# Row maxima turned as fp32, small steps of the norm on GpSimd, and repeated probabilities in 64-row halves: one change to a four-layer attention kernel

## The chip, the cores and the metric

The kernel runs on one core of one Trainium2 chip. A core has TensorE (PE, matrix products into PSUM), VectorE (DVE), ScalarE (ACT), GpSimd (POOL) and SyncE (SP, which here only issues DMAs). Each works through its own queue in order and they meet at semaphores. The metric is device microseconds for the whole program, the median of several executions; lower is better.

## What is computed

The reference applies four layers in turn, A, B, A, B, to x of 2048 tokens and 512 features. Each layer normalises its input, attends with 32 heads of 16 features, projects and adds. A looks at 8 keys per token, every second one back; B at the last 256 keys.

```python
def _A_ref(x, wqkv, wo):
    W, dil = 8, 2
    ...
    logits = jnp.einsum("bhsd,bhswd->bhsw", q, kg) * scale
    logits = jnp.where(mask[None, None, :, :], logits, -1e9)
    attn = _softmax(logits, axis=-1)
    o = jnp.einsum("bhsw,bhswd->bhsd", attn, vg)

def _B_ref(x, wqkv, wo):
    ...
    H = 32; Dh = D // H; W = 256
    ...
    mask = (idx[:, None] - idx[None, :] >= 0) & (idx[:, None] - idx[None, :] < W)
    scores = jnp.where(mask[None, None], scores, -1e9)
    p = _softmax(scores, axis=-1)
    o = jnp.einsum("bhqk,bhkd->bhqd", p, v)

x = A_x
x = x + _A_ref(_layernorm(x, axis=-1), A_wqkv, A_wo)
x = x + _B_ref(_layernorm(x, axis=-1), B_wqkv, B_wo)
x = x + _A_ref(_layernorm(x, axis=-1), A_wqkv, A_wo)
x = x + _B_ref(_layernorm(x, axis=-1), B_wqkv, B_wo)
```

Products are carried out as sums of three fp16 products: each operand is split into a high half (`xh`, `wh`) and the rest (`xl`, `wl`).

## The kernel before

The tokens are cut into 8 chunks of 256 (`C`). A chunk passes `layer_a` and `layer_b` twice, 16 pairs in all, named A0, B0 to A15, B15. Nothing is issued where it is written: `plan.add` records a task with its engine, its estimated time, the values it reads and writes, and a label of TensorE's tiling (`mode`: F the whole array, R halves of 64 rows, C strips of 32 columns, H strips of 32 rows). Each task has a number from the table `ORDER`, one list per scope. `Plan.order` sorts each engine's tasks by these numbers, so the table is the order of every engine's queue. A negative number -1-p means: the other engine named by `alt`, at place p. At each time two or three neighbouring chunks are under way together, and the table interleaves them. The scope W holds 110 tasks of three idle matmuls that only keep TensorE busy.

The tasks that matter here, with their lines:

- `norm` (L742 to L773), 32 times: VectorE takes mean and variance of both 128-token halves and adds epsilon (`stats`, three instructions per half, the last L744), GpSimd raises to the power -0.5 (`rstd`, L747), VectorE makes the shift (`shift`, L750), ScalarE normalises (`xnorm`, L763), TensorE turns the result (L767), ScalarE takes the high half (L772), VectorE the low half (L773).
- the projections: L792 to L794 (turned, `pq`), L811 to L813 (`pv` and the output `po`).
- `layer_a`: VectorE multiplies keys and queries (`prod`, L921, `alt` GpSimd), TensorE sums over the features (L929, strips of columns), a softmax follows. `spread` (L988) repeats each probability over 8 features with a 0/1 matrix `selt`: a task of four matmuls of 32 rows and 512 columns, two per output tile, four tasks per chunk. `weigh` (L1001, VectorE) multiplies with the values, `total` (L1008 to L1010 on GpSimd, L1006 on VectorE as `alt`) sums over the 8 keys. Task n of `spread` serves the 128-token half n // 2.
- `finish`: high and low half of the output (L831 ScalarE, L833 GpSimd or VectorE), the output projection, the addition to x (L839).
- `layer_b`: for each of four groups j of heads, eight times: scores of queries against keys (`sq`, L1096 and L1099, halves), then masked copy (L1115) and maximum over the keys (L1117) on VectorE. Then the maxima are split into two fp16 halves (`msplit`, L1126 and L1127, VectorE), turned on TensorE (`mrow`, L1131), copied out of PSUM (L1140, VectorE) and put by two DMAs (`mput`, L1136) into rows 48 and 49 of each half of the query stack `stk`, so that the second scores (`sk`, L1169 and L1171) come with the maximum already subtracted. ScalarE takes the exponential (L1175), GpSimd masks (L1184), TensorE multiplies with the values (`av`, L1201, strips of columns), ScalarE empties PSUM (L1236). The score tiles `sq` and `sk` share a PSUM pool of two buffers; the other PSUM tiles share four (`q_pj`).

These lines of `Plan.add` and `Plan.order` set the order of every queue:

```python
t.place, t.alt = ORDER[self.scope][self.k] if self.scope in ORDER else len(self.tasks), alt
if t.place < 0:
    (t.eng, t.us), t.place = alt, -1 - t.place
...
for q in queue.values():
    q.sort(key=lambda t: t.place, reverse=True)
```

Of the kernel before, what the change touches and what calls it, by code (L numbers as in the profile page):

```python
# [9 lines left out]
F16 = mybir.dt.float16  # L10
BF16 = mybir.dt.bfloat16
F32 = mybir.dt.float32
# [516 lines left out]
def kernel(  # L529
# [29 lines left out]
    for name, bufs in (("q_sc", 2), ("q_pj", 4)):  # L559
        pool(name, bufs, bass.MemoryType.PSUM)  # L560
    ctx.enter_context(tc.manual_schedule())


    idf = cst.tile([P, P], F32, name="idf")
    make_identity(nc, idf)
    idh = cst.tile([P, P], F16, name="idh")
    nc.vector.tensor_copy(idh, idf)
    ones = cst.tile([1, P], F32, name="ones")
    nc.gpsimd.memset(ones, 1.0)
    mhalf = cst.tile([P, 2], F32, name="mhalf")  # L570
    nc.gpsimd.memset(mhalf, -0.5)

# [777 lines left out]
```

## Time and profile before

| | |
|---|---|
| time, median of 3 executions | 1518.68 us (1513.79 to 1522.99) |
| span of the profiled execution, first to last instruction | 1515.1 us |
| time of the profiled execution around its span | not listed |
| VectorE's rows of `norm` that the diff removes (L744, L750) | 96 instructions |
| VectorE's rows of the maxima that the diff removes (L1126, L1127, L1140) | 192 instructions |
| TensorE's rows of the spreads (L988) | 256 instructions |
| TensorE's rows of the turned maxima (L1131) | 128 instructions |

How to read the lines that follow in the prediction. A row of the groups of instructions names the line, the engine, the operation, output<-input, the shapes and the count; then come the busy time in us, the mean of one in ns, and after the second bar the idle time of the engine just before them with what ended it. A row of a tile's view has minimum, median and maximum in ns. A row of the waits has the waiting engine and line, what it waited for, the total in us, how often, and the longest. A row of the timeline has the start in us, the duration, engine, line and operation. PE's matmuls overlap in the pipeline, so the step from one start to the next tells more than the duration of one.

### The profile page before, as it was taken

What the parts mean: (1) busy time and instruction counts of PE and PEld (TensorE: products, weight loads), DVE (VectorE), ACT (ScalarE), POOL (GpSimd) and SP (SyncE); (2) the same over time, 40 slices, a digit from 0 to 9 for tenths busy, and PEclk for the clock granted to TensorE, in tenths of its full rate; (3) what the DMA queues carried; (4) which work ended last, traced back from release to release, by engine and by line L of the source; (5) the groups of instructions that cost most, each with busy time, mean ns of one, the idle gap of its engine ahead of it and who ended that gap; (6) DMA issues with size and microseconds to landing.
All of it is one profiled execution on the core that took longest, in us unless ns stands there. A gap on an engine that the chain in (4) does not pass through costs nothing.

```text
span 1515.1 us, 35124 instructions
## 1 busy us (share of the span) xinstructions
PE 1394.5 (92%) x14186; PEld 793.1 (52%) x14186; DVE 1257.6 (83%) x2361; ACT 732.5 (48%) x1011; POOL 695.4 (46%) x783
## 2 busy tenths in 40 slices
PE   6899989989898998989999998999989899898988
PEld 4574636546374553736446363645637365463544
DVE  6968797987979888897988869798897979889774
ACT  6522445455455554455545344544544555445554
POOL 2504163463726356172452727255372735628232
PEclk9898989999999998999999898998999999999999
DMA  6030211222121221222112122212212121121221
GB/s 236 15 97 23 69 47 56 56 61 75 41 87 37 70 56 53 78 52 77 45 52 77 39 87 52 84 38 60 79 41 85 33 88 48 57 77 40 77 53 44
DMA packets 73091, 96.34 MB, mean 64 GB/s; under 512 B 17120, under 2 KB 44256, under 8 KB 72928
## 3 DMA queue, kind: packets, MB, share of 16 engines
q1 hardware_dynamic: 72672, 93.83, 21.5%
q8 instruction: 111, 1.82, 0.5%
q14 instruction: 52, 0.43, 0.1%
q10 hardware_dynamic: 256, 0.26, 0.1%
HBM read 49.81 MB, written 34.05 MB: 55 GB/s over the span
## 4 chain that ended last, share of the span: by engine, by line
PE 56%; DVE 19%; POOL 7%; issue 6%; ACT 5%; DMA 4%; SPq 3%; ACTq 0%; POOLq 0%; DVEq 0%
PE pq L792 9%; PE pq L793 7%; PE pq L794 7%; PE av L1201 6%; DVE m L1117 5%; PE sk L1169 4%; ACT p L1175 4%; PE L L929 3%; DVE sq L1115 3%; PE po L811 3%; PE sq L1096 3%; PE po L813 2%; PE po L812 2%; POOL pw L1008 2%; PE sq L1099 2%
## 5 line engine op out<-in xcount | busy, mean ns | idle before, releaser
L1175 ACT ACTIVATE p<-sk,sclB 128x768 f32<-128x768 f32 x480 | 426.6, 900 | 297.5 <-PE sk L1171 278.3
L1184 POOL TENSOR_SCALAR_AFFINE_SELECT p<-p 128x1024 f32<-128x1024 f32 x240 | 266.6, 1116 | 499.4 <-ACT p L1175 455.5
L1117 DVE TENSOR_REDUCE m<-sq 128x2 f32<-128x512 f32 x448 | 310.4, 693 | 15.4
L1115 DVE COPY_PREDICATED sq<-maskt,sq 128x256 f32<-128x256 int16 x448 | 188.8, 421 | 81.4 <-PE sq L1099 74.7
L1201 PE MATMUL av<-p,v 128*32 128x128 f32 (+1 forms) x3840 | 202.6, 334 | 7.4 <-POOL p L1184 7.3
L921 DVE TENSOR_TENSOR pr<-kv,q 128x512 f32<-128x512 f32 x223 | 167.4, 807 | 35.4 <-ACT q L900 17.1
L1169 PE MATMUL sk<-stk,stk 64*128 64x256 f16 x960 | 138.2, 287 | 36.8 <-DVE m L1117 20.2
L1201 PEld LDWEIGHTS av<-p,v 128*32 128x32 f32 x3840 | 109.0, 110 | 93.7 <-issue 33.3
L1001 DVE TENSOR_TENSOR pw<-pb,kv 128x1024 f32<-128x1024 f32 x128 | 153.1, 1214 | 4.0 <-POOL o L1010 1.7
L1008 POOL TENSOR_TENSOR pw<-pw 128x512 f32<-128x512 f32 x104 | 132.7, 1276 | 25.1 <-DVE pw L1001 24.4
L1096 PE MATMUL sq<-stk,stk 48*128 48x128 f16 (+1 forms) x896 | 114.5, 255 | 32.0 <-DVE m L1117 17.8
L1099 PE MATMUL sq<-stk,stk 48*128 48x256 f16 (+1 forms) x1024 | 128.4, 252 | 8.5 <-DVE m L1110 3.6
L1169 PEld LDWEIGHTS <-stk 64*128 64x128 f16 x960 | 53.3, 94 | 156.4 <-issue 99.4
L1096 PEld LDWEIGHTS <-stk 48*128 48x128 f16 x896 | 50.0, 95 | 123.1 <-issue 78.8
L1171 PE MATMUL sk<-stk,stk 64*128 64x128 f16 x960 | 109.3, 223 | 0.0
L763 ACT ACTIVATE xn<-x,rs 128x512 f32<-128x512 f32 x64 | 52.0, 813 | 80.9 <-DVE rs L750 72.9
L1009 POOL TENSOR_TENSOR pw<-pw 128x256 f32<-128x256 f32 x104 | 76.3, 734 | 8.2
L921 POOL TENSOR_TENSOR pr<-kv,q 128x512 f32<-128x512 f32 x33 | 46.5, 1415 | 58.7 <-PE L L929 36.0
L929 PE MATMUL L<-pr,sel 128*32 128x512 f32 x512 | 70.6, 601 | 0.9 <-DVE pr L921 0.7
L792 PE MATMUL pq<-xh,wA0h 128*128 128x256 f16 x256 | 70.9, 277 | 0.4 <-DVE el L1032 0.4
L792 PE MATMUL pq<-xh,wB0h 128*128 128x256 f16 x256 | 70.2, 274 | 1.0 <-DVE el L1032 1.0
L792 PE MATMUL pq<-xh,wA2h 128*128 128x256 f16 x256 | 70.6, 276 | 0.0
(183 smaller groups left out, 3159.9 us busy)
## 6 DMA issues: line engine op xcount, KB each, us to landing
stk<-re SPq DMA_DIRECT2D x256, 96.0 KB
re<-eh SPq DMA_DIRECT2D x128, 128.0 KB
re<-el SPq DMA_DIRECT2D x64, 128.0 KB
oc<-os SPq DMA_DIRECT2D x120, 64.0 KB
os<-scr SPq DMA_DIRECT2D x15, 512.0 KB
x<-in_A_x_dram SPq DMA_DIRECT2D x8, 512.0 KB
xd<-x SPq DMA_DIRECT2D x16, 256.0 KB
x<-xd SPq DMA_DIRECT2D x8, 512.0 KB
```

Source lines behind the costliest of these rows:

```text
L792: nc.tensor.matmul(ps[mp].t[:, i], wh, xh, start=k == 0, stop=False)
L921: E.tensor_mul(pr.t, window(kv[1].t, m, 64 * tq, 64)[:, 0], qb)
L1001: nc.vector.tensor_mul(pw.t, pb.t.unsqueeze(1).broadcast_to([P, 2, W, 64]), v)
L1008: E.tensor_add(t[:, :, 0:4], t[:, :, 0:4], t[:, :, 4:8])
L1096: nc.tensor.matmul(ps.t[:, par, 0 : (2 - qb) * P], lhs, stk[hf, bef][r, col, qb * P :], start=True, stop=True)
L1099: nc.tensor.matmul(ps.t[:, par, (2 - qb) * P : 3 * P], lhs, stk[hf, now][r, col, : (1 + qb) * P], start=True, stop=True)
L1115: nc.vector.copy_predicated(t[:, :, 0:P], maskt[:, 0:P].bitcast(I16).unsqueeze(1).broadcast_to([P, 2, P]), t[:, :, 2 * P : 3 * P])
L1117: nc.vector.tensor_reduce(out=m.t[:, qb, :, u], in_=t[:, :, 0 : 2 * P], op=ALU.max, axis=AX.X)
L1169: nc.tensor.matmul(o[:, two], k[:, jf * P : (jf + 1) * P], q, start=True, stop=True)
L1175: nc.scalar.activation(pt.t[:, :, 2 * i : 2 * i + 2].rearrange("p s m q -> p m s q"), ps.t[:, :, : 3 * P].rearrange("p m (s q) -> p m s q" ...
L1184: nc.gpsimd.affine_select(out=v, in_=v, pattern=[[0, 8], [-1 if b == 0 else 1, P]], compare_op=ALU.is_gt if b == 0 else ALU.is_ge, fill=0. ...
L1201: nc.tensor.matmul(o, v[:, jj, 17 * h : 17 * h + 32], rhs, start=z == 0 and (b == 0 or first), stop=z == 1 and b == 1, tile_position=(0, 3 ...
```

## The change

Five things change.

1. `norm`: `stats` loses the addition of epsilon and `shift` goes; both are done in `rstd`, which grows from one GpSimd instruction to four. The scale `XS` moves from the normalisation into the two halves that follow the turn.
2. `spread`: each matmul now contracts 64 rows instead of 32, with a table `selt` twice as large that has zeros for the rows of the other 64-token block. Task n serves both 128-token halves (`th`) of the block a = n % 2 and the group g = n // 2. Its label is R.
3. Maxima of B: `msplit` and the copy go. TensorE turns the fp32 maxima (8 rows, label F), ScalarE takes the high half out of PSUM (`mhigh`), VectorE the low half (`mlow`), and the two DMAs are two tasks, one for the high and one for the low halves, of the same number and size as before.
4. The constants `idh` and `ones` go. The idle matmuls use `selt` as weights; `ones` is a small tile made in the scope pA.
5. `ORDER` is new in all scopes; the numbers of most tasks shift a little. Some tasks change engine by their sign: on VectorE `total` 28 instead of 24, `ol` 19 instead of 7, `prod` 225 instead of 223, the scaling of B's output 17 instead of 19, `erest` 9 instead of 8; GpSimd has the rest.

```diff
--- before.py
+++ after.py
@@ -38,324 +38,326 @@
 ORDER = {
...
@@ -563,10 +565,6 @@
 
     idf = cst.tile([P, P], F32, name="idf")
     make_identity(nc, idf)
-    idh = cst.tile([P, P], F16, name="idh")
-    nc.vector.tensor_copy(idh, idf)
-    ones = cst.tile([1, P], F32, name="ones")
-    nc.gpsimd.memset(ones, 1.0)
     mhalf = cst.tile([P, 2], F32, name="mhalf")
     nc.gpsimd.memset(mhalf, -0.5)
 
@@ -605,10 +603,10 @@
                             compare_op=ALU.is_ge, fill=0.0, base=7, channel_multiplier=-1)
 
 
-    selt = cst.tile([P, 2, P], F16, name="selt")
+    selt = cst.tile([P, 2, 2, P], F16, name="selt")
     nc.gpsimd.memset(selt, 0.0)
     for tq in range(4):
-        v = selt[32 * tq : 32 * tq + 32].rearrange("p g (k d) -> p g k d", d=8)
+        v = selt[32 * tq : 32 * tq + 32, tq % 2].rearrange("p g (k d) -> p g k d", d=8)
         nc.gpsimd.affine_select(out=v, in_=v, pattern=[[-16, 2], [-1, 16], [0, 8]], compare_op=ALU.not_equal,
                                 fill=1.0, base=0, channel_multiplier=1)
 
@@ -686,8 +684,8 @@
                 nc.vector.reciprocal(a[:, 1:2], a[:, 1:2])
 
             plan.add("DVE", 1.1, one, r=[vpt], w=[va])
-            plan.add("PE", 0.3, lambda a1=a1, pt=pt: nc.tensor.matmul(pt.t[:, 2 * P : 2 * P + 2], ones, a1.t, start=True, stop=True),
-                     r=[va], w=[vpb])
+            plan.add("PE", 0.3, lambda a1=a1, pt=pt: nc.tensor.matmul(pt.t[:, 2 * P : 2 * P + 2], ones.t[0:1].rearrange("p a b -> p (a b)"), a1.t, start=True, stop=True),
+                     r=[va, vones], w=[vpb])
 
             def factors(s=s, pt=pt):
                 nc.vector.tensor_copy(psc[T, s], pt.t[:, 2 * P : 2 * P + 2])
@@ -733,7 +731,7 @@
         mv = buf("psm", [P, 2, 2], F32, "mv", f"mv{l}_{c}")
         rs = buf("psm", [P, 2, 2], F32, "rs", f"rs{l}_{c}")
         b6 = buf("psm", [P, 2, 6], F32, "b6", f"b6{l}_{c}")
-        vmv, vr0, vrs = [Val(mv), Val(mv)], [Val(rs), Val(rs), Val(rs)], Val(rs)
+        vmv, vrs = [Val(mv), Val(mv)], Val(rs)
         xh, xl = (buf("pxt", [P, 4, C], F16, n, f"{n}{l}_{c}") for n in ("xh", "xl"))
         d["xh"], d["xl"] = xh, xl
         d["vxt"] = []
@@ -741,18 +739,16 @@
         def stats(t):
             nc.vector.bn_stats(b6.t[:, t], xb.t[:, t])
             nc.vector.bn_aggr(mv.t[:, t], b6.t[:, t])
-            nc.vector.tensor_scalar(rs.t[:, 0, t : t + 1], mv.t[:, t, 1:2], 1.0e-5, 1.0 / (XS * XS), op0=ALU.add, op1=ALU.mult)
 
         def rstd():
+            nc.gpsimd.tensor_scalar(rs.t[:, 0], mv.t[:, :, 1], 1.0e-5, None, op0=ALU.add)
             nc.gpsimd.tensor_tensor(out=rs.t[:, 0], in0=rs.t[:, 0], in1=mhalf, op=ALU.pow)
-
-        def shift():
-            nc.vector.scalar_tensor_tensor(rs.t[:, 1], mv.t[:, :, 0], -1.0, rs.t[:, 0], op0=ALU.mult, op1=ALU.mult)
+            for t in range(2):
+                nc.gpsimd.tensor_scalar(rs.t[:, 1, t : t + 1], mv.t[:, t, 0:1], rs.t[:, 0, t : t + 1], -1.0, op0=ALU.mult, op1=ALU.mult)
 
         for t in range(2):
-            plan.add("DVE", 1.0, lambda t=t: stats(t), r=[vx[t]], w=[vmv[t], vr0[t], Val(b6)])
-        plan.add("POOL", 0.72, rstd, r=vr0[:2], w=[vr0[2]])
-        plan.add("DVE", 0.08, shift, r=[vr0[2], *vmv], w=[vrs])
+            plan.add("DVE", 0.93, lambda t=t: stats(t), r=[vx[t]], w=[vmv[t], Val(b6)])
+        plan.add("POOL", 1.25, rstd, r=vmv, w=[vrs])
         for t in range(2):
             pts = buf("q_pj", [P, 4, P], F32, "pj", f"pt{l}_{c}_{t}")
             xn = buf("pxn", [P, D], F32, "xn", f"xn{l}_{c}_{t}")
@@ -769,9 +765,9 @@
             sl = slice(t * P, (t + 1) * P)
             plan.add("ACT", 0.71, xnorm, r=[vx[t], vrs], w=[vxn])
             plan.add("PE", 0.48, transp, r=[vxn], w=[vpt], mode="F", act=0.213)
-            plan.add("ACT", 0.48, lambda t=t, sl=sl, pts=pts: nc.scalar.copy(xh.t[:, :, sl], pts.t), r=[vpt], w=[vh])
-            plan.add("DVE", 0.61, lambda t=t, sl=sl, pts=pts: nc.vector.tensor_sub(xl.t[:, :, sl], pts.t, xh.t[:, :, sl]),
-                     r=[vpt, vh], w=[vl])
+            plan.add("ACT", 0.49, lambda t=t, sl=sl, pts=pts: nc.scalar.activation(xh.t[:, :, sl], pts.t, AF.Copy, scale=XS), r=[vpt], w=[vh])
+            plan.add("DVE", 0.61, lambda t=t, sl=sl, pts=pts: nc.vector.scalar_tensor_tensor(
+                xl.t[:, :, sl], pts.t, XS, xh.t[:, :, sl], op0=ALU.mult, op1=ALU.subtract), r=[vpt, vh], w=[vl])
 
 
     def proj_t(l, c, s):
@@ -977,24 +973,24 @@
 
         vo = [[], []]
         for n in range(4):
-            th, g = n // 2, n % 2
+            g, a = n // 2, n % 2
             pbs = [buf("q_pj", [P, W, 64], F32, "pj", f"pb{l}_{c}_{n}_0"), buf("q_pj", [P, W, 64], F32, "pj", f"pb{l}_{c}_{n}_1")]
             vpb = [Val(x) for x in pbs]
 
-            def spread(th=th, g=g, pbs=pbs):
+            def spread(g=g, a=a, pbs=pbs):
                 for z in range(2):
-                    for a in range(2):
-                        r = slice(64 * th + 32 * a, 64 * th + 32 * a + 32)
-                        nc.tensor.matmul(pbs[a].t, selt[r, g], (half() if z else eh.t)[r], start=z == 0, stop=z == 1)
-
-            plan.add("PE", 0.5, spread, r=[veh, vel], w=vpb, mode="H", act=0.213)
-            for a in range(2):
-                pw = buf("ppw", [P, 2, W, 64], F32, "pw", f"pw{l}_{c}_{n}_{a}")
+                    for th in range(2):
+                        r = slice(64 * th, 64 * th + 64)
+                        nc.tensor.matmul(pbs[th].t, selt[r, a, g], (half() if z else eh.t)[r], start=z == 0, stop=z == 1)
+
+            plan.add("PE", 0.44, spread, r=[veh, vel], w=vpb, mode="R", act=0.43)
+            for th in range(2):
+                pw = buf("ppw", [P, 2, W, 64], F32, "pw", f"pw{l}_{c}_{n}_{th}")
                 vpw, vr = Val(pw), Val(o)
                 vo[th].append(vr)
                 t0 = 64 * (2 * th + a)
 
-                def weigh(t0=t0, g=g, pb=pbs[a], pw=pw):
+                def weigh(t0=t0, g=g, pb=pbs[th], pw=pw):
                     v = window(kv[2].t, 2 * g, t0, 64)
                     p, _, w, t = (list(x) for x in v.ap)
                     v = bass.AP(tensor=v.tensor, offset=v.offset, ap=[p, [HALO + C, 2], w, t])
@@ -1009,7 +1005,7 @@
                     E.tensor_add(t[:, :, 0:2], t[:, :, 0:2], t[:, :, 2:4])
                     E.tensor_add(to, t[:, :, 0], t[:, :, 1])
 
-                plan.add("DVE", 1.13, weigh, r=[vpb[a], *vkv[2], vhalo[2]], w=[vpw])
+                plan.add("DVE", 1.13, weigh, r=[vpb[th], *vkv[2], vhalo[2]], w=[vpw])
                 plan.add("POOL", 2.5, total, r=[vpw], w=[vr], alt=("DVE", 1.84))
         finish(l, c, o, vo)
 
@@ -1117,29 +1113,29 @@
                             nc.vector.tensor_reduce(out=m.t[:, qb, :, u], in_=t[:, :, 0 : 2 * P], op=ALU.max, axis=AX.X)
 
                     plan.add("DVE", 0.28 + 2 * (3 * P - x0) / 960 if first else 1.06, top, r=[vps], w=[v])
-            mh = buf("psm", [P, 2, 2, 2, 4], F16, "mh", f"mh{l}_{c}_{j}")
-            pm = buf("q_pj", [P, 2, P], F16, "pj", f"pm{l}_{c}_{j}")
-            mt = buf("ps1", [16, C], F16, "mt", f"mt{l}_{c}_{j}")
-            vmh, vpm, vmt = Val(mh), Val(pm), Val(mt)
-
-            def msplit(m=m, mh=mh):
-                nc.vector.tensor_scalar(mh.t[:, :, :, 0], m.t, 1.0 / MC, None, op0=ALU.mult)
-                nc.vector.scalar_tensor_tensor(mh.t[:, :, :, 1], m.t, 1.0 / MC, mh.t[:, :, :, 0], op0=ALU.mult, op1=ALU.subtract)
-
-            def mrow(mh=mh, pm=pm):
+            pm = buf("q_pj", [P, 2, P], F32, "pj", f"pm{l}_{c}_{j}")
+            mt = buf("ps1", [8, 2, C], F16, "mt", f"mt{l}_{c}_{j}")
+            vpm, vmt = Val(pm), [Val(mt), Val(mt)]
+
+            def mrow(m=m, pm=pm):
                 for qb in range(2):
-                    nc.tensor.transpose(pm.t[0:16, qb], mh.t[:, qb].rearrange("p a z m -> p (a z m)"), idh)
-
-            def mput(hf=hf, hp=hp, mt=mt):
-                for par in range(2):
-                    p0 = 64 * par + 48
-                    nc.sync.dma_start(stk[hf, 0][p0 : p0 + 2, 4 * hp : 4 * hp + 4], mt.t[8 * par : 8 * par + 8])
-
-            plan.add("DVE", 0.36, msplit, r=vm, w=[vmh], mode="S")
-            plan.add("PE", 0.2, mrow, r=[vmh], w=[vpm], mode="C")
-            plan.add("DVE", 0.2, lambda mt=mt, pm=pm: nc.vector.tensor_copy(mt.t, pm.t[0:16].rearrange("p q t -> p (q t)")),
-                     r=[vpm], w=[vmt])
-            plan.add("SP", 1.2, mput, r=[vmt], w=[vst[hf, "m", hp]], size=4)
+                    nc.tensor.transpose(pm.t[0:8, qb], m.t[:, qb].rearrange("p a u -> p (a u)"), idf)
+
+            def mhigh(pm=pm, mt=mt):
+                nc.scalar.activation(mt.t[:, 0], pm.t[0:8].rearrange("p q t -> p (q t)"), AF.Copy, scale=1.0 / MC)
+
+            def mlow(pm=pm, mt=mt):
+                nc.vector.scalar_tensor_tensor(mt.t[:, 1], pm.t[0:8].rearrange("p q t -> p (q t)"), 1.0 / MC, mt.t[:, 0],
+                                               op0=ALU.mult, op1=ALU.subtract)
+
+            plan.add("PE", 0.2, mrow, r=vm, w=[vpm], mode="F")
+            plan.add("ACT", 0.27, mhigh, r=[vpm], w=[vmt[0]])
+            plan.add("DVE", 0.36, mlow, r=[vpm, vmt[0]], w=[vmt[1]])
+            for z in range(2):
+                def mput(z=z, hf=hf, hp=hp, mt=mt):
+                    nc.sync.dma_start(stk[hf, 0][48 + z : 113 + z : 64, 4 * hp : 4 * hp + 4], mt.t[:, z])
+
+                plan.add("SP", 0.65, mput, r=[vmt[z]], w=[vst[hf, "m", hp]], size=4)
 
             acc = buf("q_pj", [P, 2, C], F32, "pj", f"av{l}_{c}_{j}")
             vacc = Val(acc)
@@ -1278,6 +1274,9 @@
 
 
     plan.begin("pA")
+    ones = buf("ps1", [P, 2, 64], F32, "rc", "ones")
+    vones = Val(ones)
+    plan.add("POOL", 0.2, lambda: nc.gpsimd.memset(ones.t, 1.0), w=[vones])
     prep("A")
     plan.begin("pB")
     prep("B")
@@ -1307,7 +1306,7 @@
 
         def idle(junk=junk):
             for _ in range(3):
-                nc.tensor.matmul(junk.t, idh, selt.rearrange("p g k -> p (g k)"), start=True, stop=True)
+                nc.tensor.matmul(junk.t, selt[:, 1, 0], selt[:, 0].rearrange("p g k -> p (g k)"), start=True, stop=True)
 
         plan.add("PE", 0.33, idle, w=[Val(junk)], mode="F", act=0.32)
     for l in (0, 2):
```

More of the change, by code (lines that the diff above doesn't have):

```diff
@@ L40 @@
 ORDER = {
[318 rows of a table removed]
+    "pA": [
+        2, 1, 0, 2, 1, 0, 1, 2, 3, 3, 7, 5, 6, 6, 4, 4, 3, 3, 5, 4, 4, 8, 7, 37, 12, 12, 15, 13, 8, 11, 5, 8, 10, 9, 10, 12, 11, 18, 19, 16, 14, 12,
+        20, 7, 14, 25, 21, 24, 33, 28, 60, 27, 36, 24, 38,
+    ],
+    "pB": [
+        10, 13, 13, 22, 34, 35, 30, 40, 35, 40, 70, 32, 57, 14, 26, 17, 25, 46, 48, 41, 63, 43, 65, 42, 64, 39, 71, 16, 36, 15, 31, 70, 67, 48, 71,
+        51, 45, 76, 43, 79, 18, 37, 11, 34, 69, 77, 54, 90, 61, 62, 56, 82, 44, 72, 18, 34, 37, 1, 23, 20, 27, 28,
+    ],
[5 rows of a table added]
+    ],
[4 rows of a table added]
+    ],
[9 rows of a table added]
+    ],
[5 rows of a table added]
+    ],
[11 rows of a table added]
+    ],
[5 rows of a table added]
+    ],
[11 rows of a table added]
+    ],
[5 rows of a table added]
+    ],
[11 rows of a table added]
+    ],
[5 rows of a table added]
+    ],
[11 rows of a table added]
+    ],
[5 rows of a table added]
+    ],
[12 rows of a table added]
+    ],
[5 rows of a table added]
+    ],
[12 rows of a table added]
+    ],
[5 rows of a table added]
+    ],
[12 rows of a table added]
+    ],
[6 rows of a table added]
+    ],
[10 rows of a table added]
+    ],
[6 rows of a table added]
+    ],
[12 rows of a table added]
+    ],
[6 rows of a table added]
+    ],
[12 rows of a table added]
+    ],
[6 rows of a table added]
+    ],
[12 rows of a table added]
+    ],
[6 rows of a table added]
+    ],
[13 rows of a table added]
+    ],
[6 rows of a table added]
+    ],
[13 rows of a table added]
+    ],
[6 rows of a table added]
+    ],
[13 rows of a table added]
+    ],
[6 rows of a table added]
+    ],
[13 rows of a table added]
+    ],
 }
```

597 rows, old and new, of the table ORDER are left out of this document.

## The prediction

> **What bounds the kernel now.** I read five views in this order: the page's busy times and chain, the granted clock, the stretches of one period each, the waits of TensorE, and the timeline of TensorE around one long wait.
>
> ```profile
> span 1515.1 us, 35124 instructions
> PE 1394.5 (92%) x14186; PEld 793.1 (52%) x14186; DVE 1257.6 (83%) x2361; ACT 732.5 (48%) x1011; POOL 695.4 (46%) x783
> PE 56%; DVE 19%; POOL 7%; issue 6%; ACT 5%; DMA 4%; SPq 3%; ACTq 0%; POOLq 0%; DVEq 0%
> core 0: 1515.1 us, clock 0.959
> 304.00:391.00 87.00, 82.27 (x889) 47.56 (x886) 73.75 (x130) 45.50 (x63) 45.53 (x50) 0.98 0.22 61
> 1174.00:1261.00 87.00, 81.02 (x877) 47.02 (x875) 75.28 (x132) 44.33 (x62) 47.14 (x52) 1.00 0.22 63
> PE sk L1169 <- DVE m L1117: 20.2, 36, 1.6
> PE sq L1096 <- DVE m L1117: 17.8, 33, 1.7
> PE sk L1169 <- ACT p L1175: 12.7, 21, 1.8
> ```
>
> TensorE is the first limit: 92% busy, and 56% of the chain that ended last. VectorE is the second, 83% busy and 19% of the chain. The two stretches (columns: length, then PE, PEld, DVE, ACT, POOL, clock) show that this holds in the middle too: of 87 us TensorE has 81 to 82 and VectorE 74 to 75. Where TensorE waits, it is mostly for the row maxima L1117 (20.2 + 17.8 us), then for the exponentials (12.7 us). ScalarE and GpSimd are half idle.
>
> The waits cost a second time. Here TensorE waited 1.36 us for a maximum, and this followed:
>
> ```profile
> 491.92 0.40 PE L1169 MATMUL sk<-stk,stk 64*128 64x256 f16 x2 [1.36 <-DVE m L1117]
> ...
> 492.36 0.61 PE L811 MATMUL po<-wA3h,oh 128*128 128x512 f16 x1
> 492.76 0.63 PE L812 MATMUL po<-wA3l,oh 128*128 128x512 f16 x1
> ...
> 495.28 0.38 PE L811 MATMUL po<-wA3h,oh 128*128 128x512 f16 x1
> 495.50 0.38 PE L812 MATMUL po<-wA3l,oh 128*128 128x512 f16 x1
> ```
>
> Between the starts of two 512-column matmuls there are 0.40 us at 492, and 0.22 us at 495: for some 3 us the array ran at half speed. The mean clock of 0.959 then means 0.041 / 0.5 = 8.2% of the span, 124 us, at half speed, and 62 us lost by it.
>
> **The change part by part.**
>
> *TensorE's tilings.* A change of tiling (whole array, 64-row halves, 32-column strips, 32-row strips) costs a gap:
>
> ```profile
> 480.39 0.38 PE L813 MATMUL pv<-wB2h,xl 128*128 128x512 f16 x1
> 480.70 0.23 PE L1096 MATMUL sq<-stk,stk 48*128 48x128 f16 x2
> ...
> 496.09 0.27 PE L1099 MATMUL sq<-stk,stk 48*128 48x256 f16 x2
> 496.20 0.28 PE L1169 MATMUL sk<-stk,stk 64*128 64x256 f16 x2
> 496.31 0.22 PE L1171 MATMUL sk<-stk,stk 64*128 64x128 f16 x2
> ```
>
> A 512-column matmul gives way to its like after 0.22 us, but to the scores in halves after 480.70 - 480.39 = 0.31 us; within one tiling (496.09 to 496.20) 256 columns take 0.11 us and nothing more. So a change costs about 0.09 us. I sorted TensorE's tasks in both order tables by their place numbers and counted neighbours with different tilings: 1387 before, 1242 after (the 128 changes around the spreads' 32-row strips go, some halves and others come back). 145 x 0.09 = **13 us less**. I counted the new fp32 turns as whole-array work, as the new code labels them; as strips, the count would be 1301 and the gain 86 x 0.09 = 8 us.
> The Trainium skill, TensorEngine Tiling (Array Packing), section Tile-to-Partition Mapping, Restrictions, says that column tiling disables the transpose of fp32 input; by that rule the count is 1242 and the gain the 13 us, without it the 8. No row of before shows an fp32 turn in a strip. Its Key Properties say that a change of the tiling mode drains the engine, and the 0.09 us agree.
>
> *The spreads' own time.*
>
> ```profile
> 481.76 0.39 PE L988 MATMUL pb<-eh,selt 32*128 32x512 f16 x2
> 481.98 0.38 PE L988 MATMUL pb<-e,selt 32*128 32x512 f16 x2
> 482.29 0.28 PE L1096 MATMUL sq<-stk,stk 48*128 48x256 f16 x2
> ```
>
> Two strips run at once and a pair takes 0.22 us. Two halves also run at once (the scores above), with the same 512 columns, so four matmuls per spread stay at 0.43 us: **0**. They fill all rows rather than half; whether that changes the clock no row shows.
>
> *The turned maxima on TensorE.*
>
> ```profile
> L1131 PE MATMUL pm<-idh,mh x128: 217/219/311, 135.1 to 1486.4; 128*16 128x128 f16 x128
> L767 PE MATMUL pt<-idf,xn x256: 272/273/476, 10.2 to 1405.0; 128*128 128x128 f32 x128
> ```
>
> These two rows have minimum, median and maximum. An fp32 turn of 128 columns takes 273 ns, an fp16 one 219: 128 x 0.054 = **7 us more**. Net on TensorE: -13 + 7 = -6 us.
>
> *VectorE.*
>
> ```profile
> L1126 DVE TENSOR_SCALAR mh<-m 128x16 f16<-128x16 f32 x64 | 24.5, 383 | 1.1
> L1127 DVE SCALAR_TENSOR_TENSOR mh<-m,mh 128x16 f16<-128x16 f32 x64 | 20.0, 313 | 2.2
> L1140 DVE COPY mt<-pm 16x256 f16<-16x256 f16 x64 | 17.4, 272 | 4.7 <-PE pm L1131 4.5
> L744 DVE TENSOR_SCALAR rs<-mv 128x1 f32<-128x1 f32 x64 | 9.8, 154 | 2.2
> L750 DVE SCALAR_TENSOR_TENSOR rs<-mv,rs 128x2 f32<-128x2 f32 x32 | 11.6, 362 | 7.3 <-POOL rs L747 7.1
> L1006 DVE TENSOR_REDUCE o<-pw 128x128 f32<-128x1024 f32 x24 | 46.1, 1921 | 0.3
> L833 DVE TENSOR_TENSOR ol<-oc,oh 128x512 f16<-128x512 f32 x4 | 2.7, 685 | 3.7 <-ACT oh L831 3.7
> ```
>
> Gone: 24.5 + 20.0 + 17.4 (maxima) + 9.8 + 11.6 (norm) = 83.3 us. New: 64 low halves of 8x256, an operation of PSUM and SBUF. It lies between the 272 ns of the copy of the same length above and the 684 ns of the same operation on 512 elements below; halving the part that grows with length I take 0.42 us, 27 us in all (ends 17 and 44).
>
> ```profile
> L1126 DVE TENSOR_SCALAR mh<-m x64: 160/175/1157, 132.6 to 1485.9; 128x16 f16<-128x16 f32 x64
> L1032 DVE SCALAR_TENSOR_TENSOR el<-pq,eh x64: 669/684/692, 87.7 to 1424.6; 128x512 f16<-128x512 f32 x64
> ```
>
> The old split needs 175 ns and sometimes 1157; the one with an operand in PSUM never leaves 669 to 692, so I add no stall.
> The Trainium skill, VectorE: DVE Perf Modes, section Why PSUM operands drop a tier, says that a PSUM operand excludes the mode that uses both SBUF read ports, and GPSIMD Engine Reference, section Specifications, that GpSimd shares those with VectorE; the spread of the two rows agrees.
>
> The new table also moves work by its negative numbers: four more of A's sums (L1006, 4 x 1.92 = 7.7) and twelve more low halves of an output (L833, 12 x 0.69 = 8.2) come to VectorE; products and B's scalings almost cancel. Net: -83 + 27 + 16 = **-40 us of VectorE**.
>
> *GpSimd and ScalarE.*
>
> ```profile
> L747 POOL TENSOR_TENSOR rs<-rs,mhalf 128x2 f32<-128x2 f32 x32 | 23.1, 721 | 84.8 <-DVE rs L744 84.7
> L892 POOL COPY kv<-ha 128x56 f32<-128x56 f32 x28 | 6.7, 249 | 0.0
> L833 POOL TENSOR_TENSOR ol<-oc,oh 128x512 f16<-128x512 f32 x28 | 32.6, 1172 | 19.2 <-ACT oh L831 17.2 <-PE pm L1131 1.7
> L1175 ACT ACTIVATE p<-sk,sclB 128x768 f32<-128x768 f32 x480 | 426.6, 900 | 297.5 <-PE sk L1171 278.3
> L1029 ACT ACTIVATE eh<-pq 128x512 f16<-128x512 f32 x64 | 37.5, 597 | 58.5 <-PE pq L794 42.4 <-DMA re<-eh 12.4 <-DMA re<-el 1.6
> PE pt L767 <- ACT xn L763: 6.3, 9, 1.2
> ```
>
> Three more tiny operations per norm, 96 in all, on GpSimd. Ends: 249 ns (a copy) and 721 (the power); these are plain arithmetic, so I take 0.25, 24 us, of which the twelve low halves that leave it (12 x 1.17 = 14) pay most. In a norm's own chain 0.75 us comes in, and 0.15 + 0.36 us and a hop back to VectorE's queue go out: no gain, no loss. Its cover is that TensorE waits only 6.3 us in all for the normalised x. Were each 0.72 us, a norm would be some 1.6 us later, 32 x 1.6 = 52 us that would then be partly bare. ScalarE gets 64 high halves of 256 elements; through 900 ns at 768 and 597 at 512 a line gives 0.30 us, 19 us in all (ends 0 and 38). ScalarE has that time, but its queue is in order: a high half that waits for its turn holds the exponentials behind it, and by the new table 34 of the 64 stand right behind an exponential. SP's transfers of the maxima are as many and as large; the high halves' now leave first. Nothing is late from `idh` and `ones`.
>
> *The sum.* Each engine's change is weighed by the share of its busy time that lies on the chain. TensorE with issue: 62 / 92 = 0.67, times -6 = -4. VectorE: 19 / 83 = 0.23, times -40 = -9. ScalarE: 5 / 48 = 0.10, times +19 = +2. GpSimd: 7 / 46 = 0.15, times +10 less four sums = +1. Together -10 us. VectorE's free share grows from 17% to 19%, so waits behind it shrink by about a tenth, as do the half-speed stretches they set off: a tenth of 62, -6 us. That makes about **-16 us**: 1515 becomes 1499 for a profiled execution. Its span lies 3.6 us under the median of 1518.68 (I know nothing else of the time around it), so I forecast about 1502 us. Bounds of the costs: all of -6 and -40 and the clock on the path, -52 us (1467); nothing on it, 1519.
>
> **The rivals.**
>
> - *No change.* The table of orders is new nearly everywhere, and TensorE runs in order: the 0.09 us saved are then spent waiting for the same maximum. For it: 81% of the chain isn't VectorE, and copy plus reduction of the scores (L1115, L1117) stay. Against it: those two engines are the chain. Time 1511 to 1526.
> - *The clock recovers.* If the freed VectorE and the full rows of the spreads take away half of the half-speed time, 31 us go instead of 6: -41 us, about 1478. For it: stretches at 1.00 exist above. Against it: the waits that set it off are only thinned.
> - *Slower: ScalarE's queue.* A high half waits for the last of eight reductions and the turn; the exponential behind it is held, with it one of the two score buffers, and TensorE stops (12.7 us of such waits already). At one reduction's length, 0.69 us, 64 of them cost 44 us, less the 16: 1547. It decides from (16 + 8) / 64 = 0.37 us bare per high half. Against it: ScalarE is idle for 52%, and the table can set the high half late.
> - *The count of tilings is wrong* (turns in column strips): 5 us less gain, within my forecast's range.
>
> **How the numbers follow.** Forecast (gain of 8 to 30 us) 0.50; clock recovers 0.14; no change 0.22; slower 0.14. A measurement of this kernel tells about 0.5% (7.6 us) from no change: faster below 1511 has 0.50 + 0.14 = 0.64, same 0.22, slower 0.14. The range goes from 1474, with most of the clock case, to 1526, the upper end of no change; outside are about 2 in 10.
>
> **What would show it.** A row of 64 low halves near 0.42 us and no `mh`; VectorE near 1217 us busy; spreads still 0.22 us apart per pair; fp32 turns at 273 ns; GpSimd's three small rows at 0.25 us; fewer waits for L1117 and a clock above 0.959. Wrong would be: ScalarE rows for `mt` with waits whose followers are the scores, small GpSimd rows near 0.7 us, or the waits for L1117 as long as before.

## The result, and the profile after

The changed kernel takes 1503.21 us (median of 4 runs, 1501.82 to 1504.43), the kernel before 1518.13 us beside it: a ratio of 0.9897, with a 95% interval of 0.9875 to 0.9919. The forecast was 1502 us. The total came out; the experiments show that not all of its terms did.

First the page and the clock of the changed kernel:

```profile
span 1502.7 us, 35144 instructions
PE 1374.5 (91%) x14186; PEld 797.5 (53%) x14186; DVE 1210.1 (81%) x2153; ACT 748.3 (50%) x1075; POOL 691.6 (46%) x854
PE 57%; DVE 15%; POOL 10%; DMA 6%; issue 5%; ACT 4%; SPq 3%; DVEq 0%; ACTq 0%; POOLq 0%
core 0: 1502.7 us, clock 0.977
```

VectorE has 47.5 us less to do (1257.6 to 1210.1) and stands on 15% of the chain, not 19%. The clock rose from 0.959 to 0.977. GpSimd's share of the chain grew from 7% to 10%, with less work than before.

TensorE's busy time fell by 20.0 us (1394.5 to 1374.5), but what the span holds beside it rose from 120.6 to 128.2 us. So TensorE's matmuls got shorter in sum; its idle time did not. Most of it is in the three rows of A's output projection, 173.1 us before and 153.9 now; the other rows moved less, up and down. One of the three, before and after (mean 453 and 406 ns):

```profile
L811 PE MATMUL po<-wA3h,oh 128*128 128x512 f16 x128 | 58.0, 453 | 0.1
```

```profile
L807 PE MATMUL po<-wA3h,oh 128*128 128x512 f16 x128 | 52.0, 406 | 0.0
```

The waits of TensorE in the changed kernel (who waited for what, us in total, times, the longest):

```profile
PE sk L1165 <- ACT p L1171: 16.6, 34, 1.1
PE sq L1092 <- ACT p L1171: 15.8, 26, 1.5
PE sq L1092 <- DVE m L1113: 14.9, 33, 1.4
PE sk L1165 <- DVE m L1113: 14.1, 30, 1.4
```

The waits for the maxima (L1117 before, L1113 now) fell from 38.0 to 29.0 us. The waits for the exponentials now come first: they rose from 24.6 to 32.4 us. The prediction shows one of the two rows before (12.7 us); the other, and ScalarE's new wait for the turned maxima, are

```profile
PE sq L1096 <- ACT p L1175: 11.9, 18, 1.8
```

```profile
ACT mt L1125 <- PE pm L1122: 35.8, 26, 3.5
```

What TensorE waits less for maxima it nearly all waits more for exponentials.

Where the time went shows in the row of the instruction that ends a layer B, with its first and last start. Before, then after:

```profile
L839 DVE SCALAR_TENSOR_TENSOR x<-po,sclB,x x32: 737/742/753, 238.4 to 1511.4; 128x512 f32<-128x512 f32 x32
```

```profile
L835 DVE SCALAR_TENSOR_TENSOR x<-po,sclB,x x32: 741/750/752, 245.0 to 1499.0; 128x512 f32<-128x512 f32 x32
```

From the first to the last there were 1273.0 us and are now 1254.0: 19 us less in the 15 periods, some 1.3 us in each. But the first comes 6.6 us later. So the gain is made period by period, and a third of it is lost at the start. There the changed kernel's timeline shows GpSimd and VectorE in the first norm of a layer B:

```profile
79.68 0.63 POOL L744 TENSOR_SCALAR rs<-mv 128x2 f32<-128x2 f32 x1 [8.47 <-DVE mv L741]
80.39 1.09 POOL L745 TENSOR_TENSOR rs<-rs,mhalf 128x2 f32<-128x2 f32 x1
81.57 2.14 POOL L747 TENSOR_SCALAR rs<-mv,rs 128x1 f32<-128x1 f32 x2
```

```profile
79.50 1.42 DVE L717 SCALAR_TENSOR_TENSOR wB0l<-stk,pscB,wB0h 128x512 f16<-128x512 f32 x2
80.82 1.45 DVE L717 SCALAR_TENSOR_TENSOR wB1l<-stk,pscB,wB1h 128x512 f16<-128x512 f32 x2
82.16 1.27 DVE L717 SCALAR_TENSOR_TENSOR wB3l<-stageB,pscB,wB3h 128x1024 f16<-128x1024 f32 x1
```

The four small steps take 81.57 + 2.14 - 79.68 = 4.0 us. Over all norms they are much shorter:

```profile
L744 POOL TENSOR_SCALAR rs<-mv x32: 222/237/627, 8.5 to 1386.4; 128x2 f32<-128x2 f32 x32
L745 POOL TENSOR_TENSOR rs<-rs,mhalf x32: 707/723/1087, 8.8 to 1386.8; 128x2 f32<-128x2 f32 x32
L747 POOL TENSOR_SCALAR rs<-mv,rs x64: 258/265/1907, 9.6 to 1388.1; 128x1 f32<-128x1 f32 x64
```

By the medians they take 0.24 + 0.72 + 2 x 0.27 = 1.5 us. Beside VectorE's splits of the weights, which read two tensors from SBUF, three of the four are stretched: to 0.63, 1.09 and 1.91 us, the longest of each row. Beside VectorE instructions with an operand in PSUM they keep their medians: with L1028 (`el`, 22 times) or L1128 (`mt`, 16 times) at their side they are at most 6 ns longer. The one other stretched step, 557 ns for 265, ran beside a low half of an output (L829 `ol`), which reads two SBUF tensors too. The Trainium skill, GPSIMD Engine Reference, section Specifications, says that GpSimd shares its SBUF interfaces with VectorE and contends with instructions of two SBUF inputs; the 4.0 us agree.

### The profile page after: what moved, and what is told of

It is laid out like the page before. It is cut to its first block, busy times and chain, and to the rows that moved or that the text cites. A ratio compares the mean times of both kernels' runs of the same rounds, so it can differ in the third digit from the quotient of the medians.

```text
span 1502.7 us, 35144 instructions
## 1 busy us (share of the span) xinstructions
PE 1374.5 (91%) x14186; PEld 797.5 (53%) x14186; DVE 1210.1 (81%) x2153; ACT 748.3 (50%) x1075; POOL 691.6 (46%) x854
## 4 chain that ended last, share of the span: by engine, by line
PE 57%; DVE 15%; POOL 10%; DMA 6%; issue 5%; ACT 4%; SPq 3%; DVEq 0%; ACTq 0%; POOLq 0%
PE pq L788 8%; PE pq L789 7%; PE pq L790 7%; PE av L1197 6%; PE sk L1165 4%; PE L L925 4%; DVE m L1113 3%; PE po L807 3%; PE sq L1092 3%; DVE pw L997 3%; POOL pw L1004 3%; PE po L809 3%; PE po L808 3%; ACT p L1171 2%; DVE sq L1111 2%
## 5 line engine op out<-in xcount | busy, mean ns | idle before, releaser
L1113 DVE TENSOR_REDUCE m<-sq 128x2 f32<-128x512 f32 x448 | 310.4, 693 | 15.4
L917 DVE TENSOR_TENSOR pr<-kv,q 128x512 f32<-128x512 f32 x225 | 158.8, 762 | 32.7 <-PE L L925 11.8
L1165 PE MATMUL sk<-stk,stk 64*128 64x256 f16 x960 | 133.9, 280 | 34.6 <-ACT p L1171 16.6
L1197 PEld LDWEIGHTS av<-p,v 128*32 128x32 f32 x3840 | 104.8, 109 | 99.2 <-issue 34.6
L1092 PE MATMUL sq<-stk,stk 48*128 48x128 f16 (+1 forms) x896 | 114.3, 252 | 33.0 <-ACT p L1171 15.8
L1004 POOL TENSOR_TENSOR pw<-pw 128x512 f32<-128x512 f32 x100 | 127.0, 1270 | 34.8 <-DVE pw L997 34.6
L1095 PE MATMUL sq<-stk,stk 48*128 48x128 f16 (+1 forms) x1024 | 126.8, 246 | 6.7 <-DVE m L1106 3.8
L917 POOL TENSOR_TENSOR pr<-kv,q 128x512 f32<-128x512 f32 x31 | 41.5, 1345 | 101.9 <-PE L L925 72.6
L1005 POOL TENSOR_TENSOR pw<-pw 128x256 f32<-128x256 f32 x100 | 72.7, 727 | 7.8
L1028 DVE SCALAR_TENSOR_TENSOR el<-pq,eh 128x512 f16<-128x512 f32 x64 | 43.5, 686 | 35.9 <-ACT eh L1025 24.2
L789 PE MATMUL pq<-xl,wA0h 128*128 128x256 f16 x256 | 70.9, 277 | 0.2 <-DVE xl L769 0.2
```

The costliest lines, as they stand in the source:

```text
L789: nc.tensor.matmul(ps[mp].t[:, i], wh, xl, start=False, stop=False)
L917: E.tensor_mul(pr.t, window(kv[1].t, m, 64 * tq, 64)[:, 0], qb)
L1004: E.tensor_add(t[:, :, 0:4], t[:, :, 0:4], t[:, :, 4:8])
L1092: nc.tensor.matmul(ps.t[:, par, 0 : (2 - qb) * P], lhs, stk[hf, bef][r, col, qb * P :], start=True, stop=True)
L1113: nc.vector.tensor_reduce(out=m.t[:, qb, :, u], in_=t[:, :, 0 : 2 * P], op=ALU.max, axis=AX.X)
L1165: nc.tensor.matmul(o[:, two], k[:, jf * P : (jf + 1) * P], q, start=True, stop=True)
```

## The experiments

Each run is compared with the kernel before on the same chip, so I give ratios; 0.001 is 1.52 us. The first four runs below share a chip. The other eight were made on two other chips, without the changed kernel beside them, and its ratio in the result (0.9897) and in the first run below (0.9870) differs by 4 us; a difference of that size between groups says little.

**The changed kernel again**, as the reference of the others.

> The changed kernel once more, beside the three that follow. 1503 us, ratio to the kernel before 0.990, clock 0.974 to 0.977. It is the reference for the runs beside it.

Measured: 1499.15 us, ratio 0.9870 (0.9851 to 0.9889). Differences of the runs in the changed kernel's order are from this ratio.

**Spreads back in 32-row strips.**

```diff
-                        r = slice(64 * th, 64 * th + 64)
+                        r = slice(64 * th + 32 * a, 64 * th + 32 * a + 32)
```

> The spreads alone go back to 32 rows each (32-row strips), in the changed kernel's order. The count of tiling changes rises from 1242 to 1326, so 84 x 0.09 = 7.6 us more of TensorE. Theory 'load of VectorE' (the clock rose because VectorE has 40 us less to do): +5 us (7.6 x 0.67), clock stays at 0.975. Theory 'full rows' (the clock rose because the spreads now fill all rows of the array): the clock falls to about 0.96 and the time rises by 20 us or more. If the tilings count for nothing: no difference.

Measured: 0.9901 (0.9884 to 0.9919), so +4.7 us, and the clock fell:

```profile
core 0: 1502.8 us, clock 0.963
```

Neither theory fits whole. The clock does fall with VectorE's work unchanged, but less than this profiled execution says: 0.963 is the lowest of five executions, up to 0.970 with a median of 0.968, against 0.974 to 0.976 in the reference. Whether the half-filled rows lower it or the 84 changes of tiling that come with the strips, this run does not separate. And that clock isn't worth what I thought: 0.012 of the span, 18 us of array time in the two profiled executions (10 us by the medians), against 4.7 us of time (0.8 to 8.6 by the two intervals), no more than the 84 changes of tiling alone explain (7.6 us, weighed 5). The pages show where the rest went: TensorE is busy for 16.9 us more (1393.1 for 1376.2) and idle for 12.4 less (109.7 for 122.1).

**The norm's small steps back on VectorE.** The shift stands 1.5 places behind the later statistics, at the latest ahead of the norm's own low half.

```diff
+            nc.vector.tensor_scalar(rs.t[:, 0, t : t + 1], mv.t[:, t, 1:2], 1.0e-5, None, op0=ALU.add)
...
-        plan.add("POOL", 1.25, rstd, r=vmv, w=[vrs])
+        plan.add("POOL", 0.72, rstd, r=vr0[:2], w=[vr0[2]])
+        plan.add("DVE", 0.08, shift, r=[vr0[2], *vmv], w=[vrs], place=...)
```

> The norm's small steps alone go back to VectorE (epsilon in the statistics, the shift as an instruction of its own one place behind them), GpSimd keeps the power; the order is otherwise that of the changed kernel. VectorE gets about 21 us more, GpSimd about 25 us less. By the share of the chain: 21 x 0.23 = +5 us. Rival from the trace at the start (the small GpSimd steps of B's first norm took 4.0 us instead of 1.3 beside VectorE's splits of the weights): the start becomes about 3 us shorter and the whole 0 to 2 us longer at most.

Measured: 0.9969 (0.9955 to 0.9983), +15.0 us; I had expected 5. The row of the layers' ends, for the reference and for this run:

```profile
L835 DVE SCALAR_TENSOR_TENSOR x<-po,sclB,x x32: 740/750/752, 245.0 to 1494.5; 128x512 f32<-128x512 f32 x32
```

```profile
L853 DVE SCALAR_TENSOR_TENSOR x<-po,sclB,x x32: 741/750/752, 240.7 to 1507.0; 128x512 f32<-128x512 f32 x32
```

The start is 4.3 us shorter, as the collision with the splits had it, and the periods are 1266.3 - 1249.5 = 16.8 us longer. In this order the small steps on GpSimd are worth over a microsecond in each period and cost 4 us once.

**The maxima back to the fp16 split.** The old code of the maxima in the changed kernel's order; the split stands half a place behind the last maximum, the copy where the low half stood.

```diff
-            plan.add("PE", 0.2, mrow, r=vm, w=[vpm], mode="F")
-            plan.add("ACT", 0.27, mhigh, r=[vpm], w=[vmt[0]])
-            plan.add("DVE", 0.36, mlow, r=[vpm, vmt[0]], w=[vmt[1]])
+            plan.add("DVE", 0.36, msplit, r=vm, w=[vmh], mode="S", place=last + 0.5)
+            plan.add("PE", 0.2, mrow, r=[vmh], w=[vpm], mode="C")
+            plan.add("DVE", 0.2, lambda ...: nc.vector.tensor_copy(...), r=[vpm], w=[vmt])
```

> The maxima alone go back to the fp16 split on VectorE ahead of the turn and the copy behind it (split right behind the last maximum, copy where the low half stood), in the changed kernel's order. VectorE +36 us, ScalarE -23 us, TensorE: 59 changes of tiling more (+5 us), turns 7 us shorter. Theory 'load of VectorE': 36 x 0.23 = +8 us and, with the clock falling towards 0.96, up to +20 us. Theory 'full rows': +5 us at most, the clock stays.

Measured: 1.0046 (1.0029 to 1.0063), +26.8 us, more than either theory gave. The clock moved little (median 0.971, for 0.9745 in the reference). One wait of TensorE is new; in the kernel before it was 1.6 us:

```profile
PE pm L1132 <- DVE mh L1128: 11.7, 16, 2.2
```

The turn stands in TensorE's queue where the new code needs it, and the split ahead of it isn't ready there. So part of the 27 us is likely VectorE's load and part a place that doesn't fit; how much of each, this run does not show.

**All three back.** All parts of the diff but the constants and the two places where a task is new, in the changed kernel's order.

> All three parts back (spreads in strips, norm's small steps and the maxima on VectorE), in the changed kernel's order: nearly the code of before in the order of after. The three alone cost 5, 15 and 27 us against the changed kernel's 1499 in that company. If the costs add up and the order was made for the new code: about 1546. If the order is as good for the old code as the old order was: about 1519, the time of before. If the new order alone had brought the gain: about 1500.

Measured: 1.0162 (1.0135 to 1.0190), +44.4 us. The three alone add up to 46.5. So the costs add within the intervals, and the old code in the new order is 1.6% slower than in its own. The new table by itself brings nothing to the old code, with the split and the shift at the places that I chose. Its first layer B ends at 247.8 us, no earlier than with the maxima alone back (247.5), so the 4 us at the start don't show in this company.

**VectorE's load alone: the low half of the maxima twice.**

```diff
+                for _ in range(2):
                     nc.vector.scalar_tensor_tensor(mt.t[:, 1], ...
```

> The low half of the maxima is computed twice in a row, 64 x 0.40 = 26 us more on VectorE, with no new wait and no other place. By the share of the chain (0.23): +6 us. If in a fixed order VectorE's time lies nearly all on the path, as 27 us for 36 us of maxima suggest (0.75): +19 us. If those 27 us came from the turn that waits for the split: +6 us or less.

Measured: 0.9964 (0.9949 to 0.9979), +14.3 us. Its group of instructions:

```profile
L1129 DVE SCALAR_TENSOR_TENSOR mt<-pm,mt 8x256 f16<-8x256 f32 x128 | 52.2, 407 | 7.7 <-ACT mt L1125 5.3
```

Against 64 of 404 ns in the changed kernel the row has 26 us more, with hardly more wait ahead of it; by the page VectorE is busy for 23.9 us more (1232.4 for 1208.5), since rows overlap. So a microsecond on VectorE costs 14.3 / 23.9 = 0.60 us (0.44 to 0.75 by the two intervals), not the 0.23 of the prediction. This price holds what the load brings with it: the low half is complete 0.4 us later, and the clock fell (median 0.971 for 0.9745), with 8.6 us more of busy time on TensorE (1384.8 for 1376.2). VectorE's share of the chain went from 13% in the reference to 20%.

**VectorE's load alone: idle steps behind the statistics.**

```diff
+            nc.vector.tensor_scalar(b6.t[:, t, 0:1], mv.t[:, t, 1:2], 1.0e-5, None, op0=ALU.add)
+            nc.vector.scalar_tensor_tensor(b6.t[:, t, 1:2], mv.t[:, t, 0:1], -1.0, mv.t[:, t, 1:2], op0=ALU.mult, op1=ALU.mult)
```

> Four idle small instructions on VectorE behind each norm's statistics (two per half, about 0.155 us each, 20 us in all), results unused; GpSimd keeps its four. It is the load of the norm's old steps without their waits and without GpSimd's relief. If the 15 us of the norm's way back were VectorE's time: +15 us. If they were the shift that waits on VectorE's queue for GpSimd: +5 us or less.

Measured: 0.9923 (0.9897 to 0.9949), +8.1 us. VectorE's busy time is 1227.6 us instead of the reference's 1208.5, 19.1 more: a slope of 0.42 (0.17 to 0.68 by the intervals, so this run alone doesn't exclude 0.23). That is over half of what the norm's way back cost (15.0); the rest is likely the shift, which waits in VectorE's queue for GpSimd.

```profile
L750 DVE SCALAR_TENSOR_TENSOR rs<-mv,rs 128x2 f32<-128x2 f32 x32 | 13.7, 428 | 5.1 <-POOL rs L754 5.1
```

Of that wait VectorE's own row with the norm back shows 5.1 us.

**Parts of the change in the old order.** Each is the kernel before, with its own table; the shift's number is skipped, the old split's too.

```diff
-        plan.add("POOL", 0.72, rstd, r=vr0[:2], w=[vr0[2]])
-        plan.add("DVE", 0.08, shift, r=[vr0[2], *vmv], w=[vrs])
+        plan.add("POOL", 1.25, rstd, r=vmv, w=[vrs])
+        plan.k += 1
```

> The kernel before in its own order, with one part of the change: the norm's small steps on GpSimd (the shift's place falls out). VectorE has 21 us less to do. If VectorE's time counts in any fixed order as it did when it was added to the changed kernel (0.5 us per us): about 10 us less than before. If only an order made for it can use it: within 3 us of before.

Measured: 0.9937 (0.9914 to 0.9961), 9.6 us less than before. The norm's part pays in an order that wasn't made for it: VectorE is busy for 17.0 us less by the page (1240.6 for 1257.6), a slope of 0.56. Here too the first layer B ends later than in the kernel before, by 3.8 us (242.2 for 238.4).

```diff
+            plan.k += 1
+            plan.add("PE", 0.2, mrow, r=vm, w=[vpm], mode="F")
+            plan.add("ACT", 0.27, mhigh, r=[vpm], w=[vmt[0]], place=HIGH[f"{plan.scope}.{j}"])
+            plan.add("DVE", 0.36, mlow, r=[vpm, vmt[0]], w=[vmt[1]])
```

> The kernel before in its own order, with the new maxima alone: no split ahead of the turn, the high half on ScalarE at the place in its queue that stood next when the old copy ran, the low half at the copy's place; the idle matmuls take their weights from selt. VectorE has 35 us less to do, TensorE 7 us more. With 0.6 us per us of VectorE: about 20 us less than before. If only an order made for it can use it: within 5 us of before. If high halves in ScalarE's queue hold the exponentials: slower than before.

Measured: 1.0119 (1.0099 to 1.0139), 18 us **more** than before, though VectorE is busy for 31.6 us less:

```profile
PE 1406.0 (92%) x14186; PEld 789.9 (51%) x14186; DVE 1226.0 (80%) x2232; ACT 750.5 (49%) x1075; POOL 693.9 (45%) x783
DVE mt L1134 <- ACT mt L1131: 40.5, 47, 2.1
```

VectorE waits 40.5 us for the high half on ScalarE, 47 times out of 64. What stands behind the low half in its queue is most often the masked copy of a score tile (30 of 64). In the changed kernel the same wait is

```profile
DVE mt L1128 <- ACT mt L1125: 5.8, 8, 1.8
```

The new table gives the high half time before VectorE comes to the low half. That this wait makes the 18 us is an argument from the trace: it is the largest wait that the kernel before doesn't have, and the places of the high halves were mine.

> Both together in the old order: VectorE has 56 us less. If the code's parts bring the gain and the order is only fitted around them: about 30 us less than before (1490), or as much as the changed kernel without its 64-row spreads (15 us less). If the new order is what brings it: within 5 us of before.

Measured: 1.0099 (1.0073 to 1.0125), 15 us more than before. The norm's gain is nearly gone beside the new wait.

**Norms at the start back on VectorE**, first three of them, then one:

```diff
+        back = l < 2 and c == 0 or l == 0 and c == 1
...
+        back = l == 1 and c == 0
```

> The norm's small steps go back to VectorE in the first three norms only (A0, B0, A1), where VectorE is splitting the weights; all 29 others stay on GpSimd. From the milestones of the run with all norms back: the start became 4.3 us shorter by the end of the first chunk and the periods after it 1.1 us longer each. So this one should keep the first and not the second: 3 to 4 us less than the changed kernel, about 1495. If the gain at the start is eaten by waits later: 1499.

Measured: 0.9859 (0.9835 to 0.9884), 1.7 us less than the reference, inside both intervals. In its profiled execution the first layer B ended 4.4 us earlier than the reference's, and the end of the last came later (1498.1 against 1494.5). That execution was the slowest of the five (1503.58 us, the median is 1500.15), so the later end may be its own; why the later periods were longer I could not tell.

> The changed kernel with the small steps of one norm only, B0's, on VectorE: the one that took 4.0 us on GpSimd beside the splits of the weights. The start should be about 3 us shorter. If the time saved at the start stays: 3 us less than the changed kernel (ratio to before 0.985). If, as with three norms back, it is lost over the later periods: no difference (0.987).

Measured: 1496.29 us, 0.9844 (0.9823 to 0.9865), 4 us less than the reference; the two intervals overlap.

```profile
L853 DVE SCALAR_TENSOR_TENSOR x<-po,sclB,x x32: 740/749/752, 241.9 to 1493.5; 128x512 f32<-128x512 f32 x32
```

The start is 3.1 us shorter, as expected, and the end of the profiled execution 1.0 earlier. It is the fastest of the kernels here, clearly ahead of the kernel before; ahead of the changed kernel by the median, not beyond doubt.

## Why the prediction was right, point by point

*What bounds the kernel.* That TensorE comes first and VectorE second held. The loads put on VectorE cost 0.42 and 0.60 us per us.

*VectorE's sum* was -40 us, worked out from rows; the rows give -51.6, and the page, where overlapping rows count once, -47.5. The low half took 404 ns (0.42 forecast) and never stalled (379 to 413). Of the surplus in the rows, 8.6 us are the products, whose row fell from 807 to 762 ns on average, 167.4 to 158.8 us in all.

*The weight of VectorE* was the step that failed: 0.23, its share of the chain over its share of the span. With the 0.42 to 0.60 that the two added loads measured, the term is -20 to -28 us rather than -9, though part of that is the clock, which the prediction counted by itself. The share of one chain says where one path ran; it doesn't say how much the end moves when an engine gets less to do. It isn't fixed either: two executions of the changed kernel gave 15% and 13%, and 2% more work on VectorE made it 20%. That paths of nearly the same length through VectorE lie beside the chain is the likely reason; no run shows it.

*The clock* came the way that was forecast, and further: 0.977 in the profiled execution, 0.974 in the other three. The thinner waits are not its only cause. With the spreads in strips and VectorE's work unchanged it was 0.968, so the spreads have a part, by the rows that they fill, for which I said that no row shows it, or by the changes of tiling beside them; with more load on VectorE alone it was 0.971, so that has one too. What failed is its price. From 0.959 to 0.977 the array gained 27 us of its time, and the whole gain is 15. In the run with strips 16.9 us more of busy TensorE cost 4.5 us of span, since 12.4 us came out of its idle time: there most of the half speed fell into time that TensorE would have spent waiting.

*The tilings and the turns* were sized right: 273 ns for the fp32 turn, as forecast, and the 84 changes around the spreads cost 4.7 us (0.8 to 8.6) where 7.6 x 0.67 = 5 was due. The spreads' own time did stay: from this row of the changed kernel's timeline to the next, 0.22 us.

```profile
312.26 0.40 PE L984 MATMUL pb<-eh,selt 64*128 64x512 f16 x2
312.48 0.39 PE L984 MATMUL pb<-e,selt 64*128 64x512 f16 x2
```

*GpSimd's small steps* at 0.25 us were right in the middle (237 and 265 ns) and wrong at the start, where they took part of 4.0 us. That "no gain, no loss" in a norm's chain missed the neighbour on VectorE: the start came out 6.6 us longer, and by the runs with norms put back 3.1 to 4.4 us of it are these steps. The rest of the 6.6 us has no run of its own.

*The slower rival*, ScalarE's queue, shows in the changed kernel, but small: ScalarE waits 35.8 us for the turn ahead of high halves, an exponential is next in its queue behind 31 of the 64 (34 forecast), and TensorE's waits for exponentials rose by 7.8 us, far from the 24 us at which this rival decides in the prediction. With the old table the new maxima cost more than everything gained, 18 us, and there the longer wait was in VectorE's queue, where the low half waits for the high half. The new table takes that wait from 40.5 to 5.8 us, and the high half takes 365 ns where I had 0.30 us.

So the sum of 16 us came out because errors met, which is luck: VectorE's two terms, -9 for its weight and -6 for the clock that its waits set off, stand against -20 to -28 by the loads, clock included, and the start, at nothing in the forecast, came 6.6 us later.

What stays open is how much of the gain is the table's and how much the code's: the old code in the new order is 24.6 us slower than in its own, the new norm and maxima in the old order 15 us slower; each belongs to the other. The 64-row spreads were not tried in the old order, since their tasks feed both token halves.

## What to carry to other kernels

Weigh an engine's saving not by its share of one chain alone, but by a load put on it: two lines that repeat an instruction give the slope. When work moves into another queue, look for the instruction that will wait for it and what stands behind that one; the new maxima were 27 us better than the old ones in the new order and 18 us worse in the old order. And ask what VectorE does beside a small step that is handed to GpSimd: here the four of a norm took 1.5 us, and 4.0 us beside instructions that read two SBUF tensors. When the clock recovers, read from the pages whether TensorE's busy time or its idle time pays for it.

## What was not expected of the hardware

The granted clock went with the form of a few matmuls: the spreads, of 512 columns each, gave 0.963 to 0.970 in strips of 32 rows and 0.974 to 0.976 in halves of 64 rows, with the same work elsewhere. Whether the filled rows did it or the 84 more changes of tiling is not shown. Counted in the traces, the runs with 1242 changes lie at medians of 0.971 to 0.977; the one with 1301, in 64-row halves too, lies at 0.971, and those with over 1380, all in strips, lie at 0.955 to 0.961. And GpSimd instructions of 0.24 to 0.72 us took 0.63 to 1.91 us while VectorE split weights, but kept their medians beside VectorE instructions with an operand in PSUM.
